# Attention with sinks feeding a two-layer expert: V's sink rows picked by TensorE, the first loads on two queues, and a plan that chooses the engine

## The chip, the cores and the metric

The kernel runs on one core of one Trainium2 chip. The core's engines are TensorE (PE, with its weight loads PEld), VectorE (DVE), ScalarE (ACT), GpSimd (POOL) and SyncE (SP), which here only issues DMAs. The metric is the device time of one execution in microseconds (us), as the median of the runs. Before the change it is 274.54 us (three runs: 274.54, 275.70, 273.16).

## The reference

Attention over 4 batches, 8 heads, 768 positions and head size 64, all in float32, then an expert of 512 to 2048 to 512 over the 3072 tokens that come out.

```python
scores = scale * np.matmul(q, k.transpose(0, 1, 3, 2))
causal = rel >= 0                                  # rel = query position - key position
stream_keep = causal & (is_sink | in_win)          # first 4 keys, or the last 64
mask = np.where(retr, full_mask, stream_mask)      # retr: heads 0, 2, 6
scores = np.where(mask[None], scores, -1000000000.0)
a = np.exp(scores - np.max(scores, axis=-1, keepdims=True))
a = a / (np.sum(a, axis=-1, keepdims=True) + 1e-09)
x = np.matmul(a, v)             # heads side by side: 3072 x 512
h = x @ w_in                    # 3072 x 2048
g = h * (1.0 / (1.0 + np.exp(-beta * h)))
out = g @ w_out                 # 3072 x 512
```

Heads 0, 2 and 6 see all earlier keys. Heads 1, 3, 4, 5 and 7 see the 64 latest keys and the four first ones, the sinks.

## The kernel before

The work is cut into eight units: a batch and a half of its queries (384). Per unit the kernel loads q, k and V in float32, casts them to bf16 (into `q2`, `k2`, `vb`), turns q and k with TensorE transposes into `QK`, and computes scores head pair by head pair (`PAIRS`) in rounds, each into a PSUM tile `sp` of two banks. ScalarE takes the exponential into `es`, VectorE multiplies by a mask (`mask_c` for the causal diagonal, `mask_s` for the window). The four sink keys of the five streaming heads are put side by side in `KS` and give one extra round, whose exponentials are `esk`.

When a unit's rounds are done, `sums` adds up the exponentials on TensorE with selection matrices (`esel`, `esel_k`) into a PSUM bank `o`. `recips` takes the reciprocal into `rec`, `split` writes it as a high and a low bf16 part into `hl`, `spread` multiplies `hl` by `sel` on TensorE so that each reciprocal stands in all 64 rows of its head, and `spread_copy` copies this on ScalarE to `R`. `pv` multiplies the exponentials with V on TensorE: from `vb`, from `vs` (the same rows shifted by 64, written by `shift_v`) and, for the sinks, from `VK`. `norm` multiplies by `R` into `xT`.

The expert runs transposed: `mm1` makes one of 16 blocks of h per step in a PSUM bank `h`, ScalarE takes a tanh (`t`), VectorE makes `gT` from both. `mm2` accumulates the 16 blocks with `w_out` for 128 tokens into a bank `o`, ScalarE copies the bank to `osb` with a factor 0.5 and SP stores it. PSUM has two tiles `sp`, two banks `h` and two banks `o`; the `o` banks serve transposes, sums, spreads and the second product alike.

`VK` holds the sink rows of V of all batches and of the five heads. Before, `load_sinks` clears a float32 buffer with VectorE and fills it by five DMAs that ScalarE issues, 4 KB each (L294 to L303); GpSimd casts it once to bf16 (L740).

The order of the work is written by a planner, `_Plan` (L49). Every step is added with a key, an engine, a cost in us, the results that it needs and gives, and the places in rings of buffers that it takes and drops. `run` keeps a clock for each engine and again and again takes the step that could start first; between equal starts the smaller key goes first. The program is emitted in the order of these planned starts, and each engine runs its instructions in that order. A step that waits therefore holds up all that stands behind it on its engine, and a DMA issue counts as a step of the engine that issues it.

The keys of unit 0 are the lowest (around -100), those of unit 1 follow; these two are "early" units, whose pairs go one by one. From unit 2 on the attention of a unit is spread over the expert steps of the units before it. Before the plan, `constants()` emits all masks and selection matrices at once. In the early units q is cast by VectorE, k by ScalarE (unit 0) or GpSimd (unit 1). Weights come in chunks of 1 MB into a ring `wf` of three, of which the sinks take one place at first, and GpSimd casts each chunk in two pieces.

The loads that SP issues first are, in this order: q and k of pairs 0 to 3, beta, then the first two chunks of w_in; ScalarE issues V of unit 0 and the five sink loads.

Of the kernel before, what the change touches and what calls it, by code (L numbers as in the profile page):

```python
# [20 lines left out]
SH = [1, 3, 4, 5, 7]  # L21
NQ = 384
# [26 lines left out]
class _Plan:  # L49
# [9 lines left out]
    def add(self, key, eng, cost, f, needs=(), gives=(), take=(), drop=(), dma=0.0, mode=None):  # L59
        self.ops.append((key, len(self.ops), eng, cost, f, tuple(needs), tuple(gives), tuple(take), tuple(drop), dma, mode))  # L60

    def run(self):
        done = {}
        left = {}
        for o in self.ops:
            left.setdefault(o[2], []).append(o)
# [4 lines left out]
        bus = 2.0  # L71
        order = []
        while any(left.values()):
            best = None
            for e, q in left.items():
                for rank, o in enumerate(q[:64]):
                    if any(n not in done for n in o[5]):
                        continue
                    if any(len(self.free[r]) < sum(1 for r2, _, _ in o[7] if r2 == r) for r, _, _ in o[7]):
                        continue  # L80
                    t = max([now[e]] + [done[n] for n in o[5]])
                    for r in {r for r, _, _ in o[7]}:
                        k = sum(1 for r2, _, _ in o[7] if r2 == r)
                        t = max(t, sorted(self.free[r])[k - 1])
                    c = (t, o[0], o[1])
                    if best is None or c < best[0]:
                        best = (c, e, o)
                    if t <= now[e]:
                        break
            if best is None:  # L90
                raise ValueError("the plan is stuck: " + str([(e, q[0][0], q[0][5], q[0][7]) for e, q in left.items() if q]))
            (t, _, _), e, o = best
            left[e].remove(o)
            key, i, _, cost, f, needs, gives, take, drop, dma, md = o
# [8 lines left out]
            now[e] = end  # L103
            if dma:
                bus = max(bus, t + 0.5) + dma
                end = bus + 1.7
            end += self.LAT[e]
            for g in gives:
                done[g] = end
# [6 lines left out]
            order.append((t, i, f))  # L116
            self.log.append((t, t + cost, e, key, gives))
        return [f for _, _, f in sorted(order, key=lambda x: x[:2])]
# [3 lines left out]
def kernel(  # L122
# [23 lines left out]
    def tpool(name, bufs, space=None):  # L146
# [4 lines left out]
        q2f=6, k2f=6, vf=3, wf=3, q2=4, k2=4, vb=2, vs=2, xT=2, gT=2, t=2, osb=3, R=1, rec=1, hl=1,  # L151
# [28 lines left out]
    beta_h = consts.tile([128, FO], F32, name="beta_h")  # L180
    sel = consts.tile([128, 8, D], BF16, name="sel")
# [7 lines left out]
    VK = consts.tile([96, 5, B, D], BF16, name="VK")  # L189
# [10 lines left out]
    def constants():  # L200
        pool.memset(warm, 0.0)
        act.activation(out=warm, in_=warm, func=AF.Exp)
        pool.memset(identf, 1.0)
        aff(identf, 1, -1, 0, 128)
        aff(identf, -1, 1, 0, 128)
        dve.tensor_copy(out=ident, in_=identf)
        pool.memset(mask_c, 1.0)
        aff(mask_c, -1, 1, 0, 128)
        odd = consts.tile([128, W], BF16, name="odd")
        even = consts.tile([128, W], BF16, name="even")  # L210
# [6 lines left out]
        for u in range(2):  # L217
            m = mask_s[u].rearrange("p (c a n) -> p c a n", a=2, n=W)
            dve.tensor_copy(out=m[:, :, 0, :], in_=even.unsqueeze(1).to_broadcast([128, CK // 2, W]))
            dve.tensor_copy(out=m[:, :, 1, :], in_=odd.unsqueeze(1).to_broadcast([128, CK // 2, W]))  # L220
        dve.memset(mask_s[0][W:2 * W, 0:W], 0.0)
        dve.memset(mask_s[0][0:SINK, W:2 * W], 1.0)
        pool.memset(esel, 0.0)
        for j in range(8):
            pool.memset(esel[:, j, :, j:j + 1], 1.0)
# [4 lines left out]

        iv = ident.rearrange("p (j a h) -> p h j a", j=4, a=4)
# [3 lines left out]
        dve.tensor_reduce(out=low, in_=iv[:, 1:2, :, :], op=ADD, axis=mybir.AxisListType.XY, negate=True)  # L235
        iv = ident.rearrange("p (g i s) -> p g i s", g=4, i=8)
        dve.tensor_reduce(out=sel_k, in_=iv[:, :, 0:2, :], op=ADD, axis=mybir.AxisListType.X)
        dve.memset(esel_k, 0.0)
        for pi in range(1, NP):
            for i, h in enumerate(PAIRS[pi]):  # L240
                if not RETR[h]:
                    c = XH.index(h)
                    dve.tensor_copy(out=esel_k[:, :, c:c + 1],
                                    in_=sel_k[0:96, pi - 1, i:i + 1].unsqueeze(1).to_broadcast([96, 4, 1]))

    SRC = {"q2": q, "k2": k}

    def load_qk(x, pi, nm):
# [3 lines left out]
        sp.dma_start(  # L252
# [41 lines left out]
    def load_sinks(eng):  # L294
        f = stg.tile([128, 2048], F32, name="wf", bufs=RINGS["wf"])
        f = f[0:96, 0:5 * B * D].rearrange("p (n b d) -> p n b d", b=B, d=D)
        held["sinks"] = f
        dve.memset(f, 0.0)
        for n_, h in enumerate(SH):
            pi, i = next((p, pr.index(h)) for p, pr in enumerate(PAIRS) if h in pr)  # L300
            r = 32 * (pi - 1) + SINK * i
            eng.dma_start(out=f[r:r + SINK, n_], in_=bass.AP(
                v.tensor, v.offset + h * S * D, [[D, SINK], [H * S * D, B], [1, D]]))  # L303
# [20 lines left out]
    def cast_w_in(s, i, eng):  # L324
        cast(eng, w_in_sb[2 * s + i], wst["i", s][:, :, i * FS:(i + 1) * FS])

    def cast_w_out(s, i, eng):
        cast(eng, w_out_sb[2 * s + i], wst["o", s][:, i * FO2:(i + 1) * FO2, :])
# [467 lines left out]
```

## Time and profile before

| | |
|---|---|
| median of the runs | 274.54 us |
| lowest, highest of three | 273.16, 275.70 us |
| profiled execution | 276.25 us |
| its span, first to last instruction | 274.3 us |
| busy: TensorE, VectorE, ScalarE, GpSimd | 244.7, 160.9, 161.7, 68.2 us |
| mean granted TensorE clock | 0.985 |
| read from HBM, written | 27.29 MB, 6.29 MB |

The profile is one execution; its times count from the start of its span. A row of instructions shows the engine, the operation, output and input by the program's names, partitions x elements and type, and how many there were. In a timeline the first two numbers are the start and the length; in a grouped row the numbers behind the bar are the busy time, the mean length in ns, and the engine's idle time just before, with what ended it. SPq and ACTq are the engines' DMA issues. All instructions of this kernel have the line of one helper (L43), so they are told apart by their names.

### The profile page before, as it was taken

Reading aid. Unit: us, or ns where it says so; the run is one execution under the profiler, and the core shown is the slowest. Engines: PE = TensorE matmul, PEld = TensorE weight load, DVE = VectorE, ACT = ScalarE, POOL = GpSimd, SP = SyncE. Lnnn points to the kernel's source line nnn. Section 1 sums busy time; section 2 is a strip of 40 time slices with the busy share of each in tenths; the row PEclk is TensorE's granted clock in tenths of the full one; section 3 lists DMA queues with packets and bytes.
Section 4 is the critical chain, followed back from the end, with each engine's and each line's share of the span. In section 5 each row is a group of like instructions: output and inputs, shape, how many; then the busy total and the mean of one; then the engine's idle time right before and its main releaser. Section 6 shows DMA issues by size and latency. Waiting matters only on the chain.

```text
span 274.3 us, 5830 instructions
## 1 busy us (share of the span) xinstructions
PE 244.7 (89%) x2301; PEld 134.6 (49%) x2301; DVE 160.9 (59%) x314; ACT 161.7 (59%) x278; POOL 68.2 (25%) x138
## 2 busy tenths in 40 slices
PE   0054769989999999999999999999999999999994
PEld 0032524644556446654655555655564465555541
DVE  4255986789877556585756546756654564434400
ACT  2074178578485874767377864775597756444521
POOL 5328973546348001290112001500000000000000
PEclk9999977999999999999999999999999999999998
DMA  7999999997597702161213000100100010110111
GB/s 223 338 294 281 313 314 390 388 239 196 137 256 212 188 1 80 57 174 39 68 34 95 38 35 8 39 5 36 42 38 13 28 41 1 41 39 38 41 76 76
DMA packets 50336, 33.97 MB, mean 124 GB/s; under 512 B 26740, under 2 KB 43140, under 8 KB 50308
## 3 DMA queue, kind: packets, MB, share of 16 engines
q1 hardware_dynamic: 47088, 32.78, 39.1%
q10 hardware_dynamic: 3220, 0.81, 1.3%
q8 instruction: 18, 0.29, 0.4%
q14 instruction: 10, 0.08, 0.1%
HBM read 27.29 MB, written 6.29 MB: 122 GB/s over the span
## 4 chain that ended last, share of the span: by engine, by line
PE 80%; DMA 7%; DVE 6%; ACT 2%; SPq 2%; issue 1%; POOL 1%; ACTq 0%; POOLq 0%
PE o L43 38%; PE h L43 31%; PE sp L43 12%; DMA wf<-in_moe_w_in_dram 4%; DMA k2f<-in_k_dram 3%; DVE hl L43 2%; SPq L43 2%; DVE es L43 1%; DVE rec L43 1%; DVE xT L43 1%; ACT es L43 1%; POOL KS L43 1%; DVE gT L43 1%; DVE q L43 0%; POOL VK L43 0%
## 5 line engine op out<-in xcount | busy, mean ns | idle before, releaser
L43 ACT ACTIVATE t<-h,beta_h 128x384 f32<-128x384 f32 x128 | 74.5, 584 | 55.5 <-PE h L43 54.5
L43 PE MATMUL h<-xT,w_in 128*128 128x384 bf16 x512 | 105.3, 330 | 0.9 <-DVE gT L43 0.8
L43 DVE SCALAR_TENSOR_TENSOR gT<-t,h 128x384 bf16<-128x384 f32 x128 | 70.2, 552 | 57.1 <-ACT t L43 56.0
L43 PE MATMUL o<-w_out,gT 128*128 128x512 bf16 x384 | 102.9, 379 | 0.0
L43 PEld LDWEIGHTS <-w_in 128*128 128x128 bf16 x512 | 47.6, 98 | 42.4 <-issue 5.7
L43 ACT ACTIVATE es<-sp 128x768 bf16<-128x768 f32 (+1 forms) x68 | 51.3, 794 | 9.7 <-PE sp L43 9.5
L43 PEld LDWEIGHTS <-gT 128*128 128x128 bf16 x384 | 36.3, 98 | 32.3 <-issue 1.3
L43 POOL CAST q<-q2f 128x384 bf16<-128x384 f32 x24 | 13.3, 557 | 86.7 <-PE o L43 51.8
L43 PE MATMUL sp<-QK 64*64 64x128 bf16 (+5 forms) x368 | 23.9, 256 | 6.8 <-ACT QK L43 3.5
L43 PEld LDWEIGHTS <-QK 64*64 64x64 bf16 (+1 forms) x368 | 11.1, 108 | 23.7 <-issue 16.8
L43 DVE COPY QK<-o 128x768 bf16<-128x768 bf16 (+1 forms) x20 | 15.9, 793 | 11.3 <-PE o L43 11.1
L43 ACT COPY R<-o 128x384 f32<-128x384 f32 x30 | 14.2, 477 | 12.6 <-PE o L43 12.6
L43 DVE TENSOR_TENSOR es<-es,mask_c 128x256 bf16<-128x256 bf16 (+2 forms) x32 | 11.9, 385 | 14.2 <-ACT es L43 13.5
L43 ACT COPY QK<-o 128x768 bf16<-128x768 bf16 (+1 forms) x20 | 13.4, 676 | 9.8 <-PE o L43 5.4
L43 ACT ACTIVATE osb<-o 128x512 f32<-128x512 f32 x24 | 14.3, 595 | 8.3 <-PE o L43 8.0
L43 PE MATMUL o<-ident,q 128*128 128x128 bf16 x96 | 11.3, 230 | 8.3 <-DVE q L43 8.0
L43 DVE TENSOR_TENSOR xT<-sp,R 128x768 bf16<-128x768 f32 x16 | 15.3, 954 | 5.1 <-PE sp L43 2.6
L43 PE MATMUL sp<-es,vb 128*64 128x64 bf16 (+3 forms) x228 | 16.6, 245 | 0.0
L43 PE MATMUL o<-ident,k 128*128 128x128 bf16 x96 | 11.3, 230 | 5.7 <-ACT k L43 5.7
L43 DVE TENSOR_TENSOR es<-es,mask_s 128x768 bf16<-128x768 bf16 (+1 forms) x24 | 13.0, 549 | 5.0 <-ACT es L43 4.3
L43 POOL CAST k<-k2f 128x384 bf16<-128x384 f32 x28 | 15.2, 551 | 0.1
L43 PEld LDWEIGHTS <-q 128*128 128x128 bf16 x96 | 7.3, 101 | 14.0 <-DVE q L43 8.0
(60 smaller groups left out, 183.0 us busy)
## 6 DMA issues: line engine op xcount, KB each, us to landing
q2f<-in_q_dram SPq DMA_DIRECT2D x32, 192.0 KB, 3.5
k2f<-in_k_dram SPq DMA_DIRECT2D x32, 192.0 KB, 5.8
out_dram<-osb SPq DMA_DIRECT2D x24, 256.0 KB, 2.0
wf<-in_v_dram SPq DMA_DIRECT2D x18, 256.0 KB, 4.0
wf<-in_moe_w_out_dram SPq DMA_DIRECT2D x4, 1024.0 KB
wf<-in_moe_w_in_dram SPq DMA_DIRECT2D x4, 768.0 KB, 7.7
wf<-in_moe_w_in_dram SPq DMA_DIRECT2D x8, 128.0 KB, 5.9
vf<-in_v_dram ACTq DMA_DIRECT2D x3, 256.0 KB, 4.5
```

The lines of the kernel that those rows point to most:

```text
L43: ins = f(*a, **k)
```

## The change

- The sink rows of V are no longer loaded. For each batch, once the first 128 rows of V are cast, `sink_rows` picks the first four rows with one TensorE matmul (`sink_sel`, 96 copies of the first rows of the identity, times 512 columns of `vb`) into a bank `o`, and `sink_copy` multiplies it on VectorE by `sink_own`, which keeps for each head its own four partitions, into a tile `VK` of that batch (two buffers).
- Unit 0's k loads and beta are issued by ScalarE, its q loads by SP; V of unit 0 moves from ScalarE to SP. The keys put V of unit 0 ahead of the first half of w_in, unit 1's loads behind that, then the rest of w_in and w_out. The ring `wf` no longer holds sinks.
- A step may name several engines with a cost for each; the plan takes the one that ends first. This is used for the early casts of q and k (GpSimd or VectorE), for `shift_v` (VectorE or GpSimd), and for the copies to `QK`, to `R` and to `osb` (ScalarE or VectorE).
- The plan has a lock: a GpSimd step, or a VectorE step marked `port`, starts only after the last such step. Between two TensorE steps it no longer counts the 0.2 us of latency.
- The constants are cut into steps with keys and are part of the plan.
- The reciprocal stays in the PSUM bank of the sums, and `split` reads it there; the bank is dropped after `split`. `R` is taken by the first `spread`.
- Weight chunks are cast in four pieces; each step of `mm1` and `mm2` needs only its own piece.

```diff
-    def add(self, key, eng, cost, f, needs=(), gives=(), take=(), drop=(), dma=0.0, mode=None):
+    def add(self, key, eng, cost, f, needs=(), gives=(), take=(), drop=(), dma=0.0, mode=None, port=False):
+        one = isinstance(eng, str)
+        alts = [(eng, cost)] if one else list(zip(eng, cost))
...
-                    t = max([now[e]] + [done[n] for n in o[5]])
+                    t = max([0.0] + [done[n][0] - (0.2 if e == "pe" and done[n][1] == e else 0.0) for n in o[4]])
...
+                    starts = {}
+                    for e2 in o[2]:
+                        starts[e2] = max(t, now[e2], lock if e2 == "pool" or (e2 == "dve" and o[10]) else 0.0)
+                    if e != min(starts, key=lambda e2: starts[e2] + o[2][e2]):
+                        continue
+                    t = starts[e]
...
+            if e == "pool" or (e == "dve" and port):
+                lock = end
...
-    def load_sinks(eng):
-        f = stg.tile([128, 2048], F32, name="wf", bufs=RINGS["wf"])
...
-        dve.memset(f, 0.0)
-        for n_, h in enumerate(SH):
...
-            eng.dma_start(out=f[r:r + SINK, n_], in_=bass.AP(
-                v.tensor, v.offset + h * S * D, [[D, SINK], [H * S * D, B], [1, D]]))
+    def sink_rows(b):
+        t = ps_o.tile([128, 512], F32, name="o")
+        pe.matmul(t[0:96, :], sink_sel, v_b[b][:, 0, :, :].rearrange("p h d -> p (h d)"), start=True, stop=True)
+        held["sinks"] = t
+    def sink_copy(b):
+        v_k[b] = vp.tile([96, H, D], BF16, name="VK", bufs=RINGS["VK"])
+        dve.tensor_mul(v_k[b], held.pop("sinks")[0:96, :].rearrange("p (h d) -> p h d", d=D),
+                       sink_own.unsqueeze(2).to_broadcast([96, H, D]))
...
     def cast_w_in(s, i, eng):
-        cast(eng, w_in_sb[2 * s + i], wst["i", s][:, :, i * FS:(i + 1) * FS])
+        c = slice(i % 2 * 128, (i % 2 + 1) * 128)
+        cast(eng, w_in_sb[2 * s + i // 2][:, :, c], wst["i", s][:, :, i * 128:(i + 1) * 128])
...
-        rec = rp.tile([96, 128], F32, name="rec")
-        dve.reciprocal(rec, x.sm[0:96, 0:128])
-        x.rec = rec
+        dve.reciprocal(x.sm[0:96, 0:128], x.sm[0:96, 0:128])
...
+        rec = x.sm[0:96, 0:128]
+        dve.tensor_copy(out=hi, in_=rec)
...
-            dve.scalar_tensor_tensor(out=hl[r, j * 128:(j + 1) * 128], in0=hi[r], scalar=low[r], in1=x.rec[r],
+            dve.scalar_tensor_tensor(out=hl[r, j * 128:(j + 1) * 128], in0=hi[r], scalar=low[r], in1=rec[r],
...
-                add(key["lq"] + 0.2 * pi, "sp", 0.47, lambda pi=pi, nm=nm: load_qk(x, pi, nm), dma=0.58,
+                e = "act" if n == 0 and nm == "k2" else "sp"
+                add(key["lq"] + 0.01 * pi, e, 0.47, lambda pi=pi, nm=nm, e=e: load_qk(x, pi, nm, ENG[e]), dma=0.58,
...
-                e = ("dve" if nm == "q2" else ["act", "pool"][u]) if early else "pool"
-                add(key["T"][pi] - 2, e, {"dve": 0.27, "act": 0.41, "pool": 0.47}[e],
-                    lambda pi=pi, nm=nm, e=e: cast_qk(x, pi, nm, ENG[e]),
+                add(key["T"][pi] - 2, ("pool", "dve") if early else ("pool",), (0.47, 0.27) if early else (0.47,),
+                    lambda e, pi=pi, nm=nm: cast_qk(x, pi, nm, ENG[e]), port=True,
...
-        add(key["cv"] + 2, "dve", 1.0, lambda: shift_v(x, dve), needs=[("v", n, j) for j in range(TU)] +
+        add(key["cv"] + 2, ("dve", "pool"), (0.9, 1.8), lambda e: shift_v(x, ENG[e]), port=True,
...
+        if not u:
+            add(key["cv"] + 3, "pe", 0.23, lambda: sink_rows(b), needs=[("v", n, 0), ("const", "sink")], gives=[("VKp", b)],
+                take=[("o", (n, "k"), 1)], drop=[("vb", b)])
+            add(key["cv"] + 3.1, "dve", 0.6, lambda: sink_copy(b), needs=[("VKp", b)], gives=[("VK", b)],
+                take=[("VK", b, 4)], drop=[("o", (n, "k"))])
...
-                for i, e in enumerate(("dve", "act")):
-                    add(k0 + 0.1, e, {"dve": 0.465, "act": 0.37}[e], lambda pi=pi, i=i, e=e: qk_copy(x, pi, ENG[e], i, 1),
+                for i in range(2):
+                    add(k0 + 0.1, ("act", "dve"), (0.37, 0.465), lambda e, pi=pi, i=i: qk_copy(x, pi, ENG[e], i, 1),
...
-            add(key["S"] + 0.4, "act", 0.37, lambda t=t: spread_copy(x, t),
+            add(key["S"] + 0.4, ("act", "dve"), (0.37, 0.465), lambda e, t=t: spread_copy(x, t, ENG[e]),
...
-            attention(n, dict(lq=-100, lv=-99, cv=-98, T=[-98, -97, -96, -95], S=-94, PV=[-93.9, -93.8]), True)
+            attention(n, dict(lq=-100, lv=-99.5, cv=-97.5, T=[-98, -97, -96, -95], S=-94, PV=[-93.9, -93.8]), True)
...
-    add(-98.5, "act", 1.6, lambda: load_sinks(act), dma=0.1, gives=[("VKf",)], take=[("wf", "k", 1)])
-    add(-96, "pool", 1.35, lambda: cast(pool, VK, held["sinks"]), needs=[("VKf",)], gives=[("VK",)],
-        drop=[("wf", "k")])
-    add(-99.1, "sp", 0.3, load_beta, dma=0.1, gives=[("beta_r",)], take=[("rec", "beta", 1)])
+    add(-99.9, "act", 0.3, load_beta, dma=0.1, gives=[("beta_r",)], take=[("rec", "beta", 1)])
...
+    add(-96.5, "dve", 0.9, const_sel, needs=[("const", "ident")], gives=[("const", "sel")])
+    add(-96.4, "dve", 1.2, const_sink, needs=[("const", "ident")], gives=[("const", "sink")])
     for s in range(NS // 2):
-        for w, k0, ld, ca in (("i", -98.5, load_w_in, cast_w_in), ("o", -80, load_w_out, cast_w_out)):
+        for w, k0, ld, ca in (("i", -99 + 0.5 * (s // 2), load_w_in, cast_w_in), ("o", -98.3, load_w_out, cast_w_out)):
```

190 lines of the change are left out of this document (104 added, 86 removed).

## The prediction

> **What bounds the kernel now.** I read the busy time by engine first, then a table of stages, then the opening of the trace instruction by instruction. The rows by stage give a stretch and its length, then the busy us (and instructions) of TensorE, its weight loads, VectorE, ScalarE and GpSimd, the granted clock, the DMA share and GB/s.
>
> ```profile
> span 274.3 us, 5830 instructions
> PE 244.7 (89%) x2301; PEld 134.6 (49%) x2301; DVE 160.9 (59%) x314; ACT 161.7 (59%) x278; POOL 68.2 (25%) x138
> ...
> 0.00:14.20 14.20, 0.50 (x3) 0.24 (x3) 4.81 (x27) 2.00 (x3) 5.92 (x28) 1.00 0.95 283
> 14.20:27.20 13.00, 6.79 (x66) 3.88 (x67) 7.25 (x16) 7.79 (x13) 7.33 (x11) 1.00 1.04 286
> 27.20:39.40 12.20, 7.94 (x124) 5.71 (x123) 10.90 (x18) 4.60 (x10) 10.78 (x17) 0.91 1.00 310
> 39.40:60.00 20.60, 19.67 (x236) 10.82 (x231) 14.74 (x28) 14.44 (x27) 9.39 (x16) 0.89 1.02 345
> 60.00:76.00 16.00, 15.16 (x149) 7.81 (x147) 13.82 (x26) 11.49 (x21) 8.90 (x16) 1.00 0.71 179
> 76.00:262.00 186.00, 186.00 (x1694) 102.43 (x1693) 109.40 (x203) 118.95 (x204) 25.92 (x55) 1.00 0.20 61
> ```
>
> TensorE idles 29.6 us of 274.3. Between 76 and 262 us it idles for nothing, at full clock: there no choice of engine can gain, only lose. From 39.4 to 76 the idle time is 1.8 us. So 24 us of the idle time lies ahead of 39.4 us, and the question is how much earlier the first expert matmul (h, at 39.41) comes. Everything behind it is a block of 274.3 - 39.4 = 234.9 us of nearly gapless TensorE.
>
> The stretch up to 39.4 us has three parts: the wait for the first scores, unit 0's attention up to its sums, and the chain from the sums to the first h.
>
> ```profile
> 1.30 0.45 SPq L43 DMA_DIRECT2D k2f<-in_k_dram  x1
> ...
> k2f<-in_k_dram SPq DMA_DIRECT2D x1, 192.0 KB, 3.5
> ...
> 6.63 1.12 DVE L43 MEMSET wf<- 96x1280 f32 x1 [0.20 <-issue]
> 8.04 5.58 ACTq L43 DMA_DIRECT2D wf<-in_v_dram  x5
> 13.66 0.51 ACT L43 CAST k<-k2f 128x384 bf16<-128x384 f32 x1 [11.36 <-DMA wf<-in_moe_w_in_dram]
> 16.43 1.51 ACT L43 ACTIVATE es<-sp 128x768 bf16<-128x768 f32 x2 [0.19 <-PE sp L43]
> ```
>
> The first k landed at 1.30 + 3.5 = 4.8 us (its last number is the time from issue to landing). ScalarE cast it only at 13.66, because five small sink loads stand ahead of the cast in ScalarE's own order and hold its queue from 8.04 to 13.62; their buffer is also cleared first by VectorE, 1.12 us. The releaser named in the cast's row, a weight load, is only the event that came last. So 8.9 us pass with k in place and nobody free to cast it.
>
> **Part by part.** *The first scores.* The sink loads, their memset and their GpSimd cast go; q and k start side by side on two queues, V's loads move behind q on SP, and the casts go to GpSimd or VectorE, whichever the plan thinks done first. k is issued at about 0.9 in place of 1.30 and lands, with the same 3.5 us, at 4.4. From cast to first exponential took 16.43 - 13.66 = 2.8 us; from 4.4 that gives 7.2 us in place of 16.43, a gain of 9.2. Bounds: 8 if the load lands no earlier and the cast runs on GpSimd behind its constants, 10 if two queues land sooner. ScalarE gets four k loads and beta to issue, at SP's half microsecond each about 2.5 us; nothing on ScalarE is wanted before 5 us, so I put that at nothing; without this cover it costs its own length.
>
> *First scores to sums.* Before, 27.24 - 16.43 = 10.8 us. What has to run there:
>
> ```profile
> L43 ACT ACTIVATE es<-sp 128x768 bf16<-128x768 f32 x6 | 4.8, 809 | 3.4 <-PE sp L43 3.3
> L43 ACT CAST k<-k2f 128x384 bf16<-128x384 f32 x4 | 2.0, 510 | 11.4 <-DMA wf<-in_moe_w_in_dram 11.4
> L43 ACT COPY QK<-o 128x384 bf16<-128x384 bf16 x4 | 1.9, 478 | 1.9 <-DVE QK L43 1.7
> ...
> L43 DVE CAST q<-q2f 128x384 bf16<-128x384 f32 x4 | 3.0, 748 | 0.0
> L43 DVE COPY QK<-o 128x384 bf16<-128x384 bf16 x4 | 2.2, 554 | 9.3 <-PE o L43 9.3
> L43 DVE TENSOR_TENSOR es<-es,mask_c 128x256 bf16<-128x256 bf16 (+2 forms) x4 | 1.8, 465 | 1.9 <-ACT es L43 1.9
> L43 DVE TENSOR_TENSOR es<-es,mask_s 128x768 bf16<-128x768 bf16 (+1 forms) x3 | 1.8, 585 | 0.0
> L43 DVE COPY vs<-vb 64x1536 bf16<-64x1536 bf16 (+2 forms) x3 | 1.2, 419 | 0.0
> ...
> L43 DVE CAST esel_k<-sel_k 96x4 bf16<-96x4 f32 x5 | 0.5, 167 | 0.0
> ```
>
> ScalarE loses its four k casts and is left with 4.8 + 1.9 = 6.7 us of work, a floor. VectorE is now the fuller one. It keeps 2.2 + 1.8 + 1.8 + 1.2 = 7.0 us; to that come two or three of the remaining six q and k casts (748 ns each beside GpSimd: 1.5 to 2.2), and the selection constants, which used to run in the idle time ahead of 7 us and have now planned places among the masks. I estimate these at 2.5 us, from five small casts that took 0.5 us together and the like; the ten that are there now are 1.0. That is 11 to 12 us of VectorE work against the 10.8 us that the stretch takes. I take 11.3, so sums at 7.2 + 11.3 = 18.5 us; the ends are 7 us (ScalarE's floor, constants off the path) and 14.5 (all casts on VectorE, all slowed).
>
> *Sums to the first h.* Before, 39.41 - 27.24 = 12.2 us:
>
> ```profile
> 27.24 2.11 PE L43 MATMUL o<-es,esel 128*32 128x128 bf16 x32
> 31.14 2.56 DVE L43 SCALAR_TENSOR_TENSOR hl<-hi,low,rec 32x128 bf16<-32x128 bf16 x3
> 35.61 0.48 ACT L43 COPY R<-o 128x384 f32<-128x384 f32 x1 [0.25 <-PE o L43]
> 38.51 0.97 PE L43 MATMUL sp<-QK 64*128 64x384 bf16 x16 [0.90 <-ACT es L43]
> 39.41 0.50 PE L43 MATMUL h<-xT,w_in 128*128 128x384 bf16 x1
> ...
> L43 DVE SCALAR_TENSOR_TENSOR hl<-hi,low,rec x3: 338/341/343, 223.9 to 224.6; 32x128 bf16<-32x128 bf16 x3
> ```
>
> The three instructions that fill hl took 2.56 us here, and 0.34 each (minimum, median, maximum in ns in the last row) late in the run, when GpSimd is idle. In the first place GpSimd was casting a weight. Now the reciprocal stays in PSUM, so they have one SBUF input instead of two. I take 3 x 0.34 = 1.03, a saving of 1.5; the bounds are 0 and 1.7, since no row shows them with a PSUM input. The Trainium skill (SBUF — State Buffer, "SBUF: two separate sides") says that VectorE and GpSimd share one port pair as an exclusive lock, taken by a VectorE operation with two SBUF inputs or in a two-port mode. The two rows agree, and by that rule the saving holds beside any GpSimd cast; without it this term is 0. The four R copies, which ended 36.1 - 33.7 = 2.4 us after hl, go to two engines: 0.9 less. The second-unit scores that TensorE took in front of h waited for an exponential; half of that microsecond and a bit of the hi cast bring 0.7. Together -3.1, so 9.1 us, and h starts at 18.5 + 9.1 = 27.6: a gain of 11.8.
>
> *What the block behind h may lack.* It starts 12 us earlier, so its weights must too.
>
> ```profile
> L43 POOL CAST w_in<-wf x8: 1036/1040/1099, 21.6 to 37.5; 128x1024 bf16<-128x1024 f32 x8
> ...
> 60.77 0.82 PE L43 MATMUL o<-w_out,gT 128*128 128x512 bf16 x3
> 260.16 10.52 PE L43 MATMUL o<-w_out,gT 128*128 128x512 bf16 x48
> ```
>
> Up to the end of w_in the queues must bring, by the shapes, 4.7 MB of q, k and V of two units and 4.2 MB of w_in: 8.9 MB, at 285 GB/s done by 31 us. With two casts of 1.04 us behind it the last quarter is there by 33. It is wanted after 12 of unit 0's 16 h steps, each four matmuls of 384 columns, by the last row (48 of 512 columns in 10.52 us) 0.66 us a step: not before 27.6 + 7.9 = 35.5, later with the scores between: covered. With w_out it is 13.1 MB, done by 44 to 46 us. Its first product moves from 60.77 to about 49: covered by 3 us, and its first quarter lands 10 us earlier. If unit 2's 2.4 MB went ahead, it would be 7 us later, and the steps that need the last quarter come after three quarters of the first 16 products, which stood among other work. I cost the earlier demand at nothing, up to 3 us without that cover. The weight casts are cut in halves, so one holds GpSimd half a microsecond instead of one; the same work.
>
> *Added work.* Four sink matmuls of 512 columns at 10.52 / 48 = 0.22 us: 0.9 us in a filled TensorE. Four VectorE products with them lie in VectorE's slack (109 us busy of 186). Against that the second unit's wait for hl, inside the 0.9 us lost between 39.4 and 60, shrinks by about 0.7. Net +0.2. The port rule and engine choice inside the plan change only the order behind 76 us: 0, bounds 0 and +1.
>
> **Sum.** 27.6 + 234.9 + 0.2 = 262.7 us of span, 11.6 less than before. The profiled execution took 276.25 us, 1.95 around its span, so it would show 264.7. The median of the runs, 274.54, lies 1.7 below the profiled one; taken off that, 274.54 - 11.6 = **263 us**. The part bounds (8 to 10, 7 to 14.5, 0 to 1.7 and a late weight of 3) allow about 257 to 268 when they do not all fall one way.
>
> **Rivals.** *More of the start goes* (chance 0.14). If the constants fall into VectorE's early gaps, ScalarE's floor holds and sums come at 7.2 + 7 = 14.2; h at 23.3, and a time of 258.6. If unit 1's scores then also fill the gap before h, two or three microseconds more go: 256. For it: TensorE itself needs only the 6.8 us that the second stage shows. Against: VectorE's list above.
>
> *The gain is given back at VectorE* (0.16). GpSimd now casts V, w_in and part of q and k in that same stretch, and each VectorE cast of q shows 748 ns beside it. Then sums come at 7.2 + 14.5 = 21.7, and with nothing saved behind them h at 33.9: a gain of 5.5, and 269.
>
> *Nothing comes of it* (0.06). If ScalarE's queue is still held, now by the k and beta loads waiting for earlier landings as the sink loads did, the first exponential stays near 14 to 16 us: 272 to 274. Against: five loads in place of eight, none behind a memset.
>
> *Slower* (0.06): the two PSUM banks named o. Sums now keep a bank until hl is written, not only to the reciprocal: 0.3 + 1.0 us longer in each of 8 units; four units also hold one for the sink product and its VectorE copy, about 1.3 us. Where the other bank holds a w_out product, transposes and spreads queue behind it, and TensorE, in order, behind those. If all of it became idle time: 8 x 1.3 + 4 x 1.3 = 15.6 us, and 263 + 15.6 = 278.6. It decides from 14 us, 1.8 us a unit. Against it: TensorE never waits from 76 us on, and h steps stand between.
>
> **How the numbers follow.** The forecast has 0.58, its own range 258 to 267. With the first two rivals' times the range is 256 to 269.5. About 1%, 2.7 us, is what a measurement of this kernel can tell from no change. Faster by more: 0.58 + 0.14 + 0.16 = 0.88; within: 0.06; slower: 0.06.
>
> **What would show it.** Right: first exponential near 7, sums near 18.5, hl three times 0.34 beside GpSimd casts, first h near 27.6, no TensorE idle behind it that was not there before. Wrong: a first exponential after 10 us; sums late with VectorE full; h waiting for w_in or the first o for w_out; new TensorE waits for bank o behind 60 us.

## The result

The changed kernel takes 265.38 us (median of four runs, 264.30 to 266.89). The kernel before, run again on the same chip, takes 274.74 us (four runs, 273.16 to 275.70). The ratio is 0.967 with a 95% interval of 0.960 to 0.974: 3.3% faster, some 9 us. The forecast was 263.0 us in a range of 256 to 269.5. The sign and the size are right, but two of the largest terms of the sum were each off by three to four us, in opposite directions. In the experiments a run that lay more than 1.5% above the fastest of its kernel is left out of the median, and no duration is read from the profile of such a run.

The profile after, first its page's head and the table of stages. The table has the same columns as in the prediction.

```profile
span 263.9 us, 5842 instructions
PE 244.3 (93%) x2277; PEld 135.8 (51%) x2305; DVE 164.1 (62%) x341; ACT 152.8 (58%) x255; POOL 72.7 (28%) x159
...
0.00:14.20 14.20, 7.21 (x69) 4.24 (x71) 9.55 (x47) 7.15 (x11) 8.01 (x35) 1.00 0.92 238
14.20:27.20 13.00, 8.81 (x106) 5.63 (x101) 8.91 (x21) 3.26 (x7) 6.85 (x13) 0.84 0.99 253
27.20:39.40 12.20, 11.09 (x106) 5.44 (x106) 9.43 (x20) 11.23 (x20) 6.27 (x10) 0.89 1.02 288
39.40:60.00 20.60, 19.06 (x250) 11.91 (x252) 14.73 (x27) 13.73 (x25) 16.87 (x35) 1.00 1.04 341
60.00:76.00 16.00, 15.53 (x159) 8.89 (x158) 13.03 (x26) 10.27 (x19) 8.73 (x16) 1.00 1.04 235
```

TensorE had 0.50 us of work in the first 14.2 us and now has 7.21; that is the gain. Two things are worse: the queues moved 238 and 253 GB/s in the first two stages against 283 and 286, and from 60 to 76 us they are now full (share 1.04 against 0.71). In this trace 28 matmul records are missing (2277 against 2305 weight loads), so its TensorE sums are too small, by some 2 us in all (244.3 against 246.1); where sums matter below, they are taken from a sister kernel whose trace is complete.

The opening of the kernel after, instruction by instruction:

```profile
7.75 1.51 ACT L42 ACTIVATE es<-sp 128x768 bf16<-128x768 f32 x2 [1.19 <-PE sp L42]
...
2.31 0.23 DVE L42 TENSOR_REDUCE sel_c<-ident 128x8 f32<-128x64 bf16 x1
4.70 0.52 DVE L42 COPY mask_s<-odd 128x192 bf16<-128x192 bf16 x1
5.14 0.34 DVE L42 CAST k<-k2f 128x384 bf16<-128x384 f32 x1
8.11 0.36 DVE L42 CAST q<-q2f 128x384 bf16<-128x384 f32 x1
...
15.35 0.29 PE L42 MATMUL o<-es,esel_k 96*32 96x128 bf16 x2 [0.82 <-ACT es L42]
15.35 1.78 PE L42 MATMUL o<-es,esel 128*32 128x128 bf16 x32
18.48 1.05 DVE L42 SCALAR_TENSOR_TENSOR hl<-hi,low,o 32x128 bf16<-32x128 bf16 x3
...
17.03 2.29 POOL L42 CAST w_in<-wf 128x512 bf16<-128x512 f32 x4 [3.08 <-DMA wf<-in_moe_w_in_dram]
21.02 2.29 POOL L42 CAST w_in<-wf 128x512 bf16<-128x512 f32 x4 [1.70 <-DMA wf<-in_moe_w_in_dram]
23.23 0.54 POOL L42 CAST q<-q2f 128x384 bf16<-128x384 f32 x1
...
23.82 0.50 PE L42 MATMUL o<-ident,q 128*128 128x128 bf16 x3 [3.37 <-POOL q L42]
24.57 1.49 PE L42 MATMUL h<-xT,w_in 128*128 128x384 bf16 x4
```

The first exponential is at 7.75 (before 16.43), the sums are at 15.35 (27.24), the first h is at 24.57 (39.41). VectorE made its constants between 2.3 and 5.2 us, until the first k was there to cast. The last five rows show the new wait. GpSimd takes the second chunk of w_in before unit 1's q; that chunk lands only at 21.0, so the q cast waits behind it, and TensorE waits 3.37 us for q.

### The profile page after: what moved, and what is told of

It is laid out like the page before. It is cut to its first block, busy times and chain, and to the rows that moved or that the text cites. A ratio compares the mean times of both kernels' runs of the same rounds, so it can differ in the third digit from the quotient of the medians.

```text
span 263.9 us, 5842 instructions
## 1 busy us (share of the span) xinstructions
PE 244.3 (93%) x2277; PEld 135.8 (51%) x2305; DVE 164.1 (62%) x341; ACT 152.8 (58%) x255; POOL 72.7 (28%) x159
## 4 chain that ended last, share of the span: by engine, by line
PE 74%; DMA 15%; POOL 4%; SPq 2%; issue 2%; ACT 0%; POOLq 0%; ACTq 0%
PE o L42 37%; PE h L42 27%; PE sp L42 10%; DMA wf<-in_moe_w_in_dram 9%; DMA wf<-in_moe_w_out_dram 4%; SPq L42 2%; DMA q2f<-in_q_dram 2%; POOL w_in L42 1%; POOL w_out L42 1%; POOL k L42 1%; POOL q L42 1%; ACT osb L42 0%; POOLq L42 0%; POOL KS L42 0%; ACTq L42 0%
## 5 line engine op out<-in xcount | busy, mean ns | idle before, releaser
L42 PE MATMUL h<-xT,w_in 128*128 128x384 bf16 x512 | 102.8, 330 | 1.1 <-DVE gT L42 1.0
L42 PE MATMUL o<-w_out,gT 128*128 128x512 bf16 x356 | 94.5, 379 | 2.7 <-issue 0.8
L42 POOL CAST q<-q2f 128x384 bf16<-128x384 f32 x28 | 15.5, 553 | 61.0 <-PE o L42 37.4
L42 ACT COPY QK<-o 128x768 bf16<-128x768 bf16 (+1 forms) x24 | 16.8, 708 | 17.9 <-PE o L42 14.4
L42 DVE TENSOR_TENSOR es<-es,mask_c 128x256 bf16<-128x256 bf16 (+2 forms) x32 | 10.9, 350 | 16.6 <-ACT es L42 16.3
L42 PE MATMUL o<-ident,q 128*128 128x128 bf16 x96 | 11.9, 239 | 8.6 <-POOL q L42 8.6
L42 ACT ACTIVATE osb<-o 128x512 f32<-128x512 f32 x19 | 11.3, 596 | 10.5 <-PE o L42 10.0
L42 PE MATMUL sp<-es,vb 128*64 128x64 bf16 (+3 forms) x228 | 17.2, 250 | 0.0
L42 POOL CAST k<-k2f 128x384 bf16<-128x384 f32 x27 | 15.2, 563 | 1.3 <-DMA k2f<-in_k_dram 1.3
L42 DVE COPY QK<-o 128x384 bf16<-128x384 bf16 (+1 forms) x16 | 11.6, 731 | 5.4 <-ACT QK L42 3.1
L42 POOL CAST vb<-wf 128x512 bf16<-128x512 f32 x18 | 10.8, 623 | 11.7 <-DMA wf<-in_v_dram 11.6
L42 PEld LDWEIGHTS <-vb 128*64 128x64 bf16 x228 | 12.7, 116 | 1.5
```

The lines of the kernel that those rows point to most:

```text
L42: ins = f(*a, **k)
```

## The experiments

Times are medians; the ratio is to runs of the kernel before on the same chip (274.4 to 274.8 us), so one hundredth is 2.75 us. Where a ratio is compared with "after", that is 0.9669; differences are taken of unrounded ratios.

### The sink loads alone, off ScalarE

```diff
-    add(-98.5, "act", 1.6, lambda: load_sinks(act), ...
+    add(-98.5, "sp", 1.6, lambda: load_sinks(sp), ...
```

> The kernel before, with one edit: SyncE instead of ScalarE issues the five sink loads. Theory (ScalarE's queue was held): the first k is cast near 7 us instead of 13.66, the first exponential comes near 10 instead of 16.4, the first h 5 to 6 us earlier than 39.4; SyncE is held by the cleared buffer until 7.8 and by five more issues, so weights come up to 2.5 us later. 268 to 270 us. Rival (the start is bound by the transfers or by VectorE, and the held queue only stood in front of that): the cast comes early but sums and h stay within 2 us of where they were, 272 to 275 us.

271.52 us, ratio 0.989 (0.986 to 0.993). ScalarE's queue and TensorE in this kernel:

```profile
6.78 0.51 ACT L43 CAST k<-k2f 128x384 bf16<-128x384 f32 x1 [4.48 <-DMA q2f<-in_q_dram]
10.56 1.51 ACT L43 ACTIVATE es<-sp 128x768 bf16<-128x768 f32 x2 [0.19 <-PE sp L43]
...
33.49 1.46 PE L43 MATMUL h<-xT,w_in 128*128 128x384 bf16 x4
```

Moving five small DMA issues to another engine brings the first k cast from 13.66 to 6.78 and the first exponential from 16.43 to 10.56. The reading that these issues held ScalarE's queue is shown. Why they took 5.58 us there isn't: on SyncE the same five took 1.65 us (from 7.79). Of the 5.9 us by which the first h comes earlier, the span (270.8) keeps 3.5. This was the first sign that an early h is partly paid back.

### After, with every cast and copy on its former engine

```diff
-                add(key["T"][pi] - 2, ("pool", "dve") if early else ("pool",), ...
+                ce = ("dve" if nm == "q2" else ["act", "pool"][u]) if early else "pool"
+                add(key["T"][pi] - 2, (ce,), ...
```

The other steps with a choice were fixed in the same way (`shift_v`, the copies to `QK`, `R` and `osb`).

> The changed kernel with every copy and cast back on the engine that it had before (k of unit 0 on ScalarE, q on VectorE, R and osb on ScalarE). Theory (the start is gained by freeing the queue, the choice of engine adds little): sums of unit 0 up to 1.5 us later than 15.35, 265 to 267.5 us. Rival (the choice is what shortened the way from the first exponential to the sums and from the sums to h): sums 3 us or more later, 269 us or more.

270.93 us, ratio 0.986 (0.980 to 0.992). The choice of engine is worth (0.986 - 0.967) x 274.8 = 5 us of the 9. I had expected most of the gain without it. Where the 5 us are lost isn't shown, since only times are used here.

### After, with the reciprocal in SBUF again

```diff
-        dve.reciprocal(x.sm[0:96, 0:128], x.sm[0:96, 0:128])
+        x.rec = rp.tile([96, 128], F32, name="rec")
+        dve.reciprocal(x.rec, x.sm[0:96, 0:128])
```

> The changed kernel with the reciprocal written to SBUF as before. Theory: the three hl instructions of unit 0 take 2 to 2.6 us instead of 1.05 beside GpSimd's weight casts, but h then comes at most 0.5 us later, since TensorE waits for unit 1's q until 23.8 in any case: 265 to 266.5 us. Rival (hl's length is on the path): 1.5 us or more, 267 us and more.

266.35 us, ratio 0.970 (0.966 to 0.973). The filling of `hl` in this kernel, and the wait behind it:

```profile
18.43 1.55 DVE L42 SCALAR_TENSOR_TENSOR hl<-hi,low,rec 32x128 bf16<-32x128 bf16 x3
...
20.04 0.48 PE L42 MATMUL o<-hl,sel 96*128 96x384 bf16 x2 [0.43 <-DVE hl L42]
```

With two SBUF inputs the three instructions take 1.55 us beside the w_in casts, with one PSUM input 1.05. So the PSUM reciprocal is worth 0.5 us at this place, not 1.5, and on the time it can't be told from nothing. The rest of the old 2.56 us was gone before it: the GpSimd casts beside it are now half as long (0.57 in place of 1.04 us). That the shorter casts are the cause is argued from the two rows, not tried by itself.

This kernel's trace is complete, and its plan is otherwise that of the kernel after. It serves below for the accounts.

### After, with unit 1's q and k cast by VectorE alone

```diff
-                add(key["T"][pi] - 2, ("pool", "dve") if early else ("pool",), ...
+                add(key["T"][pi] - 2, ("dve",) if n == 1 else ("pool", "dve") if early else ("pool",), ...
```

> The changed kernel with unit 1's q and k cast by VectorE alone. Theory (TensorE waits from 20.4 to 23.8 because unit 1's first q, landed near 21.3, stands behind weight casts in GpSimd's order): transposes of unit 1 start 1 to 2 us earlier, and 263 to 264.5 us. Rival (the landing of unit 1's q and k is the limit, whoever casts): 265 to 266 us.

267.33 us, ratio 0.976 (0.969 to 0.982): not faster. The 3.37 us wait goes and the first h starts at 22.26, but TensorE then waits for `xT` and `gT`, because VectorE has the casts to do as well:

```profile
22.26 0.48 PE L42 MATMUL h<-xT,w_in 128*128 128x384 bf16 x2 [1.87 <-DVE xT L42]
23.50 0.80 PE L42 MATMUL h<-xT,w_in 128*128 128x384 bf16 x2 [0.75 <-DVE xT L42]
```

The theory that this one wait costs its own length falls. The first h came 2.3 us earlier without it, and the time didn't.

### After, with TensorE kept busy in the wait

```diff
+    def keep_warm():
+        t = ps_h.tile([128, 512], F32, name="h")
+        for _ in range(9):
+            pe.matmul(t[:, 0:NQ], ident, QK[0][0][:, 0, 0:NQ], start=True, stop=True)
+    add(-93.5, "pe", 1.5, keep_warm, needs=[("sb", 0, t) for t in range(NP)], ...
```

The nine products are never read.

> The changed kernel with nine matmuls of 384 columns added, whose result nobody reads, in TensorE's wait from 20.5 to 23.8 us. Theory (the h steps from 24.6 to 30 us run at half clock because TensorE waited before, and this is part of what was given back): four h matmuls take 0.8 instead of 1.49 us at once, 2 to 2.7 us less, 262.7 to 263.5 us. Rival (in that stretch ScalarE, busy for 11.2 of 12.2 us, or the landing of unit 1's loads sets the pace): the matmuls are faster, waits grow by as much, 265 to 266 us.

265.34 us, ratio 0.966 (0.963 to 0.970): no change. The edit did what it says, and the time it freed went into other waits:

```profile
20.85 1.62 PE L42 MATMUL h<-QK,ident 128*128 128x384 bf16 x9 [0.46 <-ACT R L42]
24.07 0.81 PE L42 MATMUL h<-xT,w_in 128*128 128x384 bf16 x4
...
37.03 0.34 PE L42 MATMUL o<-ident,q 128*128 128x128 bf16 x3 [1.54 <-POOL q L42]
43.82 0.34 PE L42 MATMUL o<-ident,k 128*128 128x128 bf16 x3 [1.10 <-POOL k L42]
```

The first h step now takes 0.81 us, not 1.49, and no slice shows a lowered clock. But from 37 to 44 us TensorE waits 2.6 us for GpSimd's casts of unit 2, where the kernel after waits 0.9. The half clock alone isn't what holds the time.

### After, with a slower bus in the plan

```diff
-                bus = max(bus, t + 0.5) + dma
+                bus = max(bus, t + 0.5) + 1.35 * dma
```

> The changed kernel with every transfer costed 1.35 times as long in the plan, and nothing else. Theory (the plan believes that the second chunk of w_in lands at 17.7 us, it lands at 20.9, so that GpSimd stands waiting in front of unit 1's q): an order that fits the real landings, 262 to 264 us. Rival (the order is as good as any, the transfers themselves are late): 265 to 267 us.

267.36 us, ratio 0.972 (0.968 to 0.976): a plan that expects later landings is, if anything, worse. Sums come at 16.37, the first h at 24.17, and unit 1's transposes only behind the first h steps (27.92).

### After, with a quarter of the weights loaded and cast

```diff
-    for s in range(NS // 2):
+    for s in range(1):
         for w, k0, ld, ca in (("i", ...), ("o", ...)):
```

Three quarters of w_in and w_out are neither loaded nor cast; the products read the first quarter four times.

> The changed kernel with only the first quarter of w_in and of w_out loaded and cast, and used in place of the others, so the output is not the reference's; it saves 6.3 MB of transfers and 24 casts. Theory (the time given back behind the first h comes from transfers and GpSimd being full up to 60 us): unit 1's q is cast some 5 us earlier, the waits for weights go, 258 to 261 us. Rival (weights are covered, as the prediction's sum has it): 264 to 265.5 us.

260.25 us, ratio 0.947 (0.943 to 0.951): 5 us faster than after, though the first h comes no earlier. What stands ahead of h is different:

```profile
21.06 0.50 PE L42 MATMUL o<-ident,q 128*128 128x128 bf16 x3
...
23.81 0.33 PE L42 MATMUL o<-ident,k 128*128 128x128 bf16 x3
...
24.79 0.82 PE L42 MATMUL h<-xT,w_in 128*128 128x384 bf16 x4
```

All four pairs of unit 1 are now transposed between 21.06 and 24.1, in the time in which the kernel after waits for GpSimd.

### After, with all weights loaded and a quarter cast

```diff
-            for i in range(4):
-                add(k0 + 0.01 * s, "pool", 0.58, lambda s=s, i=i, ca=ca: ca(s, i, pool), needs=[("wf", w, s)], ...
+            for i in range(1 if s else 4):
+                add(k0 + 0.01 * s, "pool", 0.1 if s else 0.58, lambda s=s, i=i, ca=ca: ca(s, i, pool), needs=[("wf", w, s)], ...
```

For the later chunks a cast touches 32 elements a partition; the products read the first quarter, as above.

> The kernel after with all weight loads issued as they are, but only the first quarter of w_in and of w_out cast whole; of each other chunk GpSimd casts 32 elements a partition, so that it still waits for the chunk in its order. The products read the first quarter again and again, so the output is not the reference's. With a quarter both loaded and cast the time was 260.25 (ratio 0.9472), with everything 265.4. Theory A (GpSimd's time for the casts, 24 casts of about 0.57 us, is what holds unit 1 and the weights back): nearly all of that gain comes, 260 to 261.5, with unit 1's transposes ahead of the first h and no TensorE wait for GpSimd's q. Theory B (the transfers themselves hold it: later chunks and unit 2's q, k and V arrive too late, and GpSimd waits for them in its order): 263.5 to 266, with GpSimd idle but waiting for DMA in front of unit 1's and unit 2's casts. Between these, 262 to 263: both.

263.62 us, ratio 0.960 (0.956 to 0.965). Of the 5.4 us that the quarter brought, 1.8 come by leaving out the casts alone; the intervals of this kernel and of after overlap, so that part isn't separated from nothing. The other 3.6 us, whose intervals are apart (0.947 and 0.960), need the transfers gone too. GpSimd's rows here say why:

```profile
21.49 0.21 POOL L42 CAST w_in<-wf 128x32 bf16<-128x32 f32 x1 [2.18 <-DMA wf<-in_moe_w_in_dram]
23.94 0.51 POOL L42 CAST k<-k2f 128x384 bf16<-128x384 f32 x1 [2.23 <-DMA k2f<-in_k_dram]
...
42.23 0.21 POOL L42 CAST w_in<-wf 128x32 bf16<-128x32 f32 x1 [4.29 <-DMA wf<-in_moe_w_in_dram]
```

With hardly any casting to do, GpSimd still stands 2 to 4 us at a chunk until it lands, and unit 1's k itself lands behind the weights.

### After, with a quarter loaded and all of it cast

The loads are those of the quarter, and all 32 casts are made, from the first chunk.

```diff
+            if s == 0:
                 add(k0, "sp", ..., lambda s=s, ld=ld: ld(s), dma=2.9, gives=[("wf", w, 0)], ...)
```

> The changed kernel with only the first quarter of w_in and w_out loaded, but all 32 casts made (from that quarter, so the output is not the reference's): GpSimd's work stays, 6.3 MB of transfers go. Theory (the transfers are what is late): the whole gain of the kernel with a quarter of the weights stays, 260 to 261 us. Rival (GpSimd's casts, in order in front of unit 1's and 2's q and k, are what is late): no more than 1.5 us of it stays, 263.8 to 265.5 us.

267.80 us, ratio 0.974 (0.969 to 0.978). That is 2 us above after, but the intervals overlap. With its inputs there at once, the plan put all 32 weight casts on GpSimd in one row, ahead of unit 1's q. So this doesn't separate transfers from casts as I had meant it to. What it shows comes from the kernel with a quarter loaded and cast, whose transfers are the same: 24 more casts in that place cost (0.974 - 0.947) x 274.6 = 7 us. GpSimd's casts can therefore hold the time by themselves, when they stand ahead of unit 1's.

### After, with V of unit 0 issued by ScalarE again

```diff
-                add(key["lv"] + 0.1 * j, "sp", 1.0, lambda j=j: load_v(x, j, sp), dma=1.2,
+                ve = "sp" if n else "act"
+                add(key["lv"] + 0.1 * j, ve, 1.0, lambda j=j, ve=ve: load_v(x, j, ENG[ve]), dma=1.2,
```

> The changed kernel with V of unit 0 issued by ScalarE as before. Theory (one queue moves the first loads at 238 GB/s, two moved them at 283, since V's short pieces hold up what is behind them): unit 1's q lands 1 to 2 us earlier, 263.5 to 264.8 us. Rival (the mix of sizes sets the rate, not the queue; ScalarE is held by the issues as before): no gain in rate, 265.5 to 268 us.

269.86 us, ratio 0.983 (0.978 to 0.987), 4 us slower than after. Two stages and ScalarE's opening:

```profile
0.00:14.20 14.20, 3.54 (x37) 2.32 (x37) 6.60 (x42) 4.33 (x7) 4.90 (x29) 1.00 0.95 248
14.20:27.20 13.00, 8.19 (x117) 5.65 (x112) 9.14 (x18) 3.62 (x5) 10.22 (x19) 1.00 1.08 308
...
5.45 4.37 ACTq L42 DMA_DIRECT2D vf<-in_v_dram  x3
9.85 0.48 ACT L42 COPY QK<-o 128x384 bf16<-128x384 bf16 x1 [7.03 <-DMA k2f<-in_k_dram]
11.52 1.51 ACT L42 ACTIVATE es<-sp 128x768 bf16<-128x768 f32 x2 [1.19 <-PE sp L42]
```

The rate of the second stage goes up from 253 to 308 GB/s, but three V issues hold ScalarE from 5.45 to 9.82, and the first copy to `QK` stands behind them. The start of unit 0 loses more (the first exponential at 11.52, not 7.75) than the faster transfers give.

The theory spoke of one queue in the kernel after and two before. The rows of ScalarE's queue in the whole execution (packets, MB, share), first before, then after, say otherwise:

```profile
q10 hardware_dynamic: 3220, 0.81, 1.3%
q10 hardware_dynamic: 1120, 0.79, 1.1%
```

It carried as much in both, V and the sinks before, k and beta after, and nearly all of it in the first 14.2 us. In the second stage it carried less than 0.01 MB before, nothing after and 0.12 MB here, and the rates were 286, 253 and 308 GB/s. So the number of queues doesn't account for the fall from before to after.

### After, with weight casts on GpSimd or ScalarE, and with unit 1's loads ahead of w_in

```diff
-                add(k0 + 0.01 * s, "pool", 0.58, lambda s=s, i=i, ca=ca: ca(s, i, pool), needs=...
+                add(k0 + 0.01 * s, ("pool", "act"), (0.58, 0.6), lambda e, s=s, i=i, ca=ca: ca(s, i, ENG[e]), needs=...
```

> The changed kernel with the weight casts on GpSimd or ScalarE, as the plan finds better. If GpSimd's order is what is late, unit 1's q no longer stands behind w_in and 1.5 to 3 us go: 262.5 to 264 us. If the transfers are, it stays at 265 to 266.5 us, or loses where a cast on ScalarE waits for a weight in front of an exponential.

266.70 us, ratio 0.974 (0.968 to 0.980): no gain. Unit 1's transposes come at 22.19, ahead of h, which then starts at 26.58.

```diff
-            attention(n, dict(lq=-98.8, lv=-98.7, ...
+            attention(n, dict(lq=-99.2, lv=-98.7, ...
```

> The changed kernel with one key altered: q and k of unit 1 are loaded ahead of w_in and not behind its first half. Theory (what was given back is unit 1's attention, pushed behind the first h because its q and k landed at 21 us and later): its transposes and first scores run in the wait ahead of h, as in the kernel with a quarter of the weights; h near 25, 261.5 to 264 us. Rival (the sum of the transfers up to w_out is what binds, whatever their order): the time returns as waits for w_in or w_out, 265 to 267 us.

267.52 us, ratio 0.974 (0.969 to 0.978): no gain either. Unit 1's q and k are there in time (the first h starts at 27.10), and the weights late:

```profile
47.10 2.29 POOL L42 CAST w_in<-wf 128x512 bf16<-128x512 f32 x4 [5.47 <-DMA wf<-in_moe_w_in_dram]
...
50.91 1.70 PE L42 MATMUL o<-w_out,gT 128*128 128x512 bf16 x3 [1.88 <-POOL w_out L42]
```

The wait has moved from unit 1's q to the first use of w_out.

## Why the prediction was right, and where it was wrong

**First scores: right.** Forecast 7.2, measured 7.75, a gain of 8.7 in place of 9.2. The mechanism, DMA issues that hold ScalarE's queue, is shown from both sides: without the sink loads' issues in the old kernel k is cast 6.9 us earlier, and with V's issues put back on ScalarE the new kernel loses its start again.

**First scores to sums: mis-sized.** I took 11.3 us; it took 15.35 - 7.75 = 7.6. The step that failed is "the selection constants ... have now planned places among the masks. I estimate these at 2.5 us". The plan put them, and the window masks, between 2.3 and 5.2 us, where VectorE had nothing else. A part of the other 1.2 us: three casts of q and k in this stretch took 0.36 us each, 1.1 in all, where I put 1.5 to 2.2. The 748 ns that I used is a mean of casts from 0.35 to 1.34 us, and the longest of them ran beside a GpSimd cast; in the kernel after GpSimd cast nothing from 6.9 to 10.7 us. VectorE was busy for 6.1 of these 7.6 us, ScalarE for 6.0, and the sums waited last for ScalarE's exponentials (0.82 us). The upper end that I gave, 14.5, adds up to 14.0 from its terms. My rival "more of the start goes" had this as its condition, with sums at 14.2.

**Sums to first h: right in length, not in its parts.** Forecast 9.1, measured 24.57 - 15.35 = 9.2. `hl` took the 1.05 us that I had put, though only 0.5 of the saving is due to the PSUM input. By the rule of the Trainium skill that the prediction named (SBUF — State Buffer, "SBUF: two separate sides"), the pair of rows, 1.55 with two SBUF inputs and 1.05 with one, agrees with a lock that a VectorE operation with two SBUF inputs needs. In place of what was saved there came the 3.37 us wait for unit 1's q, which I had not named. With unit 1 cast by VectorE, and so without that wait, h started at 22.26, 6.9 us behind the sums. That the length came out at 9.2 is luck.

Together the first h came 14.8 us earlier, not 11.8.

**The block behind h: wrong.** The step that failed is "I cost the earlier demand at nothing, up to 3 us without that cover", with 0.2 us for added work. The block grew from 234.9 to 263.9 - 24.57 = 239.3 us, 4.4 in place of 0.2. The kernel with the reciprocal in SBUF (block 239.65, complete records) shows of what this consists. First the kernel before up to its first h, then that kernel in stages:

```profile
0.00:39.41 39.41, 15.24 (x194) 9.84 (x194) 22.97 (x60) 14.40 (x26) 24.04 (x55) 0.97 0.99 292
```

```profile
0.00:24.85 24.85, 13.36 (x159) 8.85 (x160) 17.07 (x62) 8.82 (x14) 13.93 (x46) 0.97 0.97 250
24.85:39.40 14.55, 13.47 (x115) 6.48 (x113) 11.03 (x24) 12.54 (x22) 7.28 (x13) 0.81 1.06 272
39.40:60.00 20.60, 18.72 (x245) 11.37 (x244) 14.85 (x26) 13.56 (x24) 17.21 (x35) 1.00 1.02 331
60.00:76.00 16.00, 15.76 (x146) 8.88 (x144) 13.35 (x27) 10.02 (x19) 8.15 (x15) 1.00 1.09 246
76.00:250.00 174.00, 174.00 (x1602) 95.63 (x1601) 107.92 (x204) 104.94 (x176) 26.62 (x53) 1.00 0.24 69
...
sum 264.50, PE 246.12 PEld 135.88 DVE 165.14 ACT 152.69 POOL 73.19; mean PE 41.02 PEld 22.65 DVE 27.52 ACT 25.45 POOL 12.20
```

- Before, TensorE did 15.24 us of work ahead of its first h, now 13.36. The long wait of old had room for unit 1's transposes and scores; the shorter one has less, and what no longer fits stands behind h: 1.9 us.
- TensorE's work in all is 246.1 us, before 244.7: 1.4 more. I had forecast 0.9, the sink products. What it consists of isn't shown: the busy time of like work is not the same in every kernel. With the sink loads off ScalarE it is 246.0 without any sink product, and with V's issues on ScalarE it is 244.0 with all of them.
- Idle time behind h is 239.65 - (246.12 - 13.36) = 6.9 us against 234.9 - (244.7 - 15.24) = 5.4: 1.5 more.

Together 4.8 us. Behind 76 us TensorE is as full as before (174.00 of 174), and all of the difference lies ahead of it. So the time is decided by how much TensorE has left to do at 76 us. The same account for other kernels, each up to its first h and from there to 76 us, the first two rows of the one with a quarter of the weights, the last two of the one that loads all and casts a quarter:

```profile
0.00:24.79 24.79, 15.72 (x181) 10.41 (x181) 19.17 (x68) 12.11 (x21) 11.94 (x43) 1.00 1.01 271
24.79:76.00 51.21, 49.46 (x531) 28.04 (x530) 36.83 (x72) 38.42 (x64) 30.71 (x53) 1.00 1.00 242
```

```profile
0.00:26.55 26.55, 16.12 (x174) 9.88 (x174) 18.17 (x68) 11.57 (x20) 11.31 (x42) 0.94 0.98 246
26.55:76.00 49.45, 47.16 (x512) 26.72 (x511) 35.52 (x72) 35.05 (x60) 20.52 (x46) 0.96 1.01 289
```

| kernel | first h at | TensorE work ahead of h | work done by 76 us | work in all | left at 76 us | span |
|---|---|---|---|---|---|---|
| before | 39.41 | 15.2 | 50.1 | 244.7 | 194.6 | 274.3 |
| sink loads off ScalarE | 33.49 | 17.2 | 55.4 | 246.0 | 190.6 | 270.8 |
| after, reciprocal in SBUF | 24.85 | 13.4 | 61.3 | 246.1 | 184.8 | 264.5 |
| all loaded, a quarter cast | 26.55 | 16.1 | 63.3 | 246.5 | 183.2 | 262.9 |
| a quarter loaded and cast | 24.79 | 15.7 | 65.2 | 244.1 | 178.9 | 258.7 |

76 us, what is left and another 3.7 to 4.2 us at the end give each span. What is done by 76 us is no measure by itself, since the work in all differs too.

The first h is thus not the whole measure that I made of it. With a quarter of the weights h starts where it does in the kernel after, 5 us are won all the same, and the block is 233.9 us: no longer than before the change. Against the third row it is 5.7 us shorter: 2.4 us more of the work stands ahead of h, TensorE's work in all is 2.0 less, and the idle time behind h is 1.4 less. So in the changed kernel the loads and casts of three quarters of the weights, which I had costed at nothing, cost about 5 us, more than my bound of 3. How much of this the kernel before paid already is open, since that kernel was not run with a quarter of the weights.

What I missed is the place where it is paid. I asked whether h or w_out would wait for its weights. They hardly do: in the kernel after, TensorE's longest waits from 24.5 to 76 us are these.

```profile
PE h L42 <- DVE gT L42: 1.0, 2, 0.7
PE o L42 <- POOL k L42: 0.9, 2, 0.6
PE o L42 <- POOL w_out L42: 0.6, 3, 0.2
```

It is paid by what queues behind the weights: GpSimd stands at each chunk until it lands and then casts it for 2.3 us, and the q and k of units 1 and 2 are cast by the same engine and come over the same transfers. The terms under it were off too. I had 285 GB/s, from the old rows, and w_in cast by 33 us; it was 238, 253 and 288 GB/s by stage, and the last chunk was cast from 41.46 to 43.75.

Why the rate fell isn't settled. The number of queues isn't what changed from before to after, as the rows of ScalarE's queue show; the mix and the order of the transfers changed too, and neither was tried alone.

**Which edits made the gain.** Taking the sink loads off ScalarE alone gives 3 us of the 9. Taking the choice of engine out of the full change costs 5. The PSUM reciprocal gives 0.8 by the ratios, which isn't separated from nothing. These are not to be added up; they overlap in the same 24 us. The constants inside the plan, its lock, V ahead of w_in and the casts in four pieces were not taken out singly.

**The sum.** The span came at 263.9 where the working gave 262.7. That it was so near is in part luck: the start came 3.0 us better than I had it, the block behind it 4.2 us worse. The other 1.2 us of the 2.4 between forecast and median are the step from span to median. I took the median of the new kernel to be 0.3 above its span, as in the kernel before, whose profiled execution lay 1.7 us above its median; it is 1.5.

**The rivals.** "More of the start goes" happened as a mechanism, but its 258.6 us did not follow, for the block's sake. "The gain is given back at VectorE" didn't happen. "Nothing comes of it" fell: ScalarE's k issues end at 4.3 us. "Slower", by the o banks, left no trace: in the rows above TensorE works 174.00 of 174 us from 76 us on.

What stays open: how the transfers act, through GpSimd's waiting or through the late landing of unit 1's and 2's q, k and V. With most of the casts gone and the transfers kept, 3.6 us of the 5.4 remained, and these go with the transfers. That GpSimd's casts can hold as much by themselves is shown by the kernel with all 32 in one row. Three changes of order (unit 1 first, casts shared with ScalarE, unit 1's casts on VectorE) each moved the wait to another place and won nothing, and no version with the full computation beat the kernel after.

## What to carry to other kernels

Look for DMA issues that hold the queue of an engine that also computes; here five of 4 KB held the first exponential back by 6 us. When a start is shortened, list the work that the old wait was hiding, on every engine and on the queues, for it must then be paid in the open: here 4.4 of 14.8 us were taken back, and about 2 of them are unit 1's work, which the old wait had covered. And where TensorE is gapless behind some point, compare kernels by the work that it has left at that point, not by when one instruction starts.

## What the runs showed of the hardware

- The granted clock of the first stage is given as 1.00, and yet three transposes of the same size take 0.50 us at 21.06 and 0.33 at 23.81 us in the kernel with a quarter of the weights, whose clock is 1.00 in every stage. In that kernel all such transposes up to 21.06 us, from the first at 5.20, take 0.50 to 0.53, and in a row they start 0.32 us apart (8.25, 8.57, 8.89), later 0.17 (21.56, 21.73). TensorE was slow there for its first 16 us without the record saying so. The Trainium skill (TensorE: Matmul & The Clock Gate, "Part 1: The HAM clock gate (the "warmup" mystery)") has the throttled state as the one in which the engine starts, released by sustained activity; the durations agree, the clock record of this case doesn't show it.
- The first two stages moved 283 and 286 GB/s before, 238 and 253 after, and 248 and 308 with V on ScalarE's queue, at a share of the engines' time of 0.92 to 1.08 each time. I had not expected the rate to differ at the same share.
